# Pooled attention and two MoE layers on one core: the float32 value products of two key tiles issued together

## The chip, the cores and the metric

The kernel runs on one core of a Trainium2 chip. The metric is the device time of one execution in microseconds; less is better. The engines of the core work side by side, each with its own queue in program order, and meet at semaphores: TensorE (PE; its weight loads appear as PEld), VectorE (DVE), ScalarE (ACT), GpSimd (POOL) and SyncE (SP), which here issues the DMAs.

## What is computed

Four batches of eight heads, 1152 keys, head size 64. Pairs of neighbouring queries are averaged, so a head has 576 queries. Then two MoE-like layers follow on the 2304 tokens of 512 features.

```python
def _attn_ref(q, k, v):
    q_pool = q.reshape(B, H, S // 2, 2, D).mean(axis=3)
    scores = scale * np.matmul(q_pool, k.transpose(0, 1, 3, 2))
    scores = scores - np.max(scores, axis=-1, keepdims=True)
    attn = np.exp(scores)
    attn = attn / (np.sum(attn, axis=-1, keepdims=True) + 1e-09)
    return np.matmul(attn, v)

def reference(...):
    x = attn_out.transpose(0, 2, 1, 3).reshape(B * S, H * D)   # S = 576 here
    x = _moe_ref(x, w_in, w_out)      # h = x @ w_in; g = h - tanh(h); g @ w_out
    return _moe2_ref(x, ...)          # g = h * sigmoid(1.702 h)
```

## The kernel before, in words

**Tiles.** The 32 heads are worked on in 16 pairs. A head's keys are nine tiles of 128 (t = 0 to 8), its 576 queries two halves of 288. A loop of 288 steps (`g`, 18 to a pair, nine to a head) computes for one key tile the scores, and three steps later (`LAG = 3`) that tile's products with the values. In this text step i of a pair is `g % 18`, and m = 0 to 8 is the step of a head counted by its value products: m = 0 is step 3 of a pair for the even head and step 12 for the odd one; m = 4 is step 7 or 16.

**Precision.** Most products are fp32r, and what one of them loses is made up by a second and third one: a value v is held as `vh + vl`, a probability p as `ph + pl`, and `vh*ph`, `vl*ph` and `vh*pl` are accumulated: six products for a tile (three parts, two halves). Every third tile (`whole(t)`, t = 1, 4, 7) instead multiplies float32 by float32 in one go (L469, `vfs` by `pf`): two products for a tile, no `ph` and no `pl`.

**One step, in order of issue.** (1) `scores(g)`: four products (L433, L434) into one of two PSUM tiles `sc`; ACT then writes `pf` (L439) and, for a tile that isn't whole, `ph` (L449). (2) `max_at[g]`: two products into the PSUM tile `mx` (L327), for the maxima of the next pair's queries; VectorE reduces `mx` (L331). The pool `ps_mx` has one buffer, so the next step's two products wait for this reduction. In steps with two such jobs the second comes after the value products. The last pair has none. (3) `rest(g - 1)`: `pl = pf - ph` of the tile before, on VectorE (L457), or on GpSimd in steps 5 and 14 of a pair's tiles (others in pair 0, none in the last pair). (4) `pv(g - 3)`: the value products of one tile. (5) the jobs of `plan` (`opening` for pair 0): among them `max_rows` in steps 3 and 13 (VectorE, L390 and L392, then DMAs), `prep_ql` in step 14 (VectorE, L294), `prep_kl` in steps 16 and 17 (GpSimd, L307), `prep_qs` in step 17 (VectorE, L283). (6) from pair 8 on, conversions of the MoE weights (`early`): in pairs 8, 10, 12 and 13 VectorE's L138 in step 6 and L158 in step 15.

Program order is the order in which each engine runs its part. PSUM is full: four banks of `sc`, two of `mx`, two of value accumulators `pv`. Buffers in SBUF: `pf` five, `ph` four, `pl` three.

Of the kernel before, what the change touches and what calls it, by code (L numbers as in the profile page):

```python
# [7 lines left out]
F32 = mybir.dt.float32  # L8
# [20 lines left out]
def tile_pooled_attention_two_moe(  # L29
# [13 lines left out]
    B, NPB, _, S = k.shape  # L43
    NT, DM = out.shape
    D = 64
    SP = S // 2
    HB = SP // 2
    KT = S // 128
# [163 lines left out]
    def attention(ctx: ExitStack):  # L212
        ap = ctx.enter_context(tc.tile_pool(name="attn", bufs=1))
# [15 lines left out]
        def whole(t):  # L229
            return t % 3 == 1  # L230
# [190 lines left out]
        probs, accs, halves = {}, {}, {}  # L421

        def scores(g):
            hd, t = divmod(g, KT)
            a1, a2, q2, q3 = stacks[hd % 3]
            pf = ap.tile([128, SP], F32, tag="pf", name="pf", bufs=5)
            ks = slice(128 * t, 128 * t + 128)
            sc = ps_sc[g % 2].tile([128, 2, 512], F32, tag="sc", name="sc")
            for x in range({1: 2, 2: 2, 3: 1}.get(g, 0)):
                nc.tensor.matmul(sc[:, x], *zeros, start=True, stop=True)  # L430
            for x in range(2):
                xs = slice(x * HB, (x + 1) * HB)
                nc.tensor.matmul(sc[:, x, 0:HB], a1[:, ks], q2[:, xs], start=True, stop=False)  # L433
                nc.tensor.matmul(sc[:, x, 0:HB], a2[:, ks], q3[:, xs], start=False, stop=True)  # L434

            def both(tile):
                return tile.rearrange("p (x i) -> p x i", x=2)

            nc.scalar.activation(both(pf), sc[:, :, 0:HB], AF.Exp, scale=SCALE)  # L439
            if whole(t):  # L440
                probs[g] = None, None, pf
                return
            ph = ap.tile([128, SP], F32R, tag="ph", name="ph", bufs=4)
            pl = ap.tile([128, SP], F32R, tag="pl", name="pl", bufs=3)
            if g in pool_cast:
                nc.gpsimd.tensor_scalar(
                    out=ph, in0=pf, scalar1=1.0, scalar2=1.0, op0=ALU.mult, op1=ALU.mult)
            else:
                nc.scalar.activation(both(ph), sc[:, :, 0:HB], AF.Exp, scale=SCALE)  # L449
            probs[g] = ph, pl, pf  # L450

        def rest(g):
            ph, pl, pf = probs[g]
            if ph is None:
                return
            eng = nc.gpsimd if g % NS in pool_sub.get(g // NS, (5, 14)) else nc.vector
            eng.tensor_tensor(pl, pf, f32(ph[:]), op=ALU.subtract)  # L457

        def pv(g):
            hd, t = divmod(g, KT)  # L460
            p, s = divmod(hd, 2)
            ph, pl, pf = probs.pop(g)
            vh, vl = vt[hd % 3]
            if t == 0:
                accs[hd] = [
                    ps_pv.tile([128, HB], F32, tag=f"pv{x}", name=f"pv{x}") for x in range(2)]
            if ph is None:
                for x in range(2):
                    nc.tensor.matmul(  # L469
                        accs[hd][x], vfs[hd % 3][:, t // 3, :], pf[:, x * HB:(x + 1) * HB],  # L470
                        start=False, stop=False)
                return
            order = [(n, x) for n in range(3) for x in range(2)]
            if t in (0, KT - 1):
                order.sort(key=lambda nx: nx[1])
            parts = (vh, ph), (vl, ph), (vh, pl)
            for n, x in order:
                w, r = parts[n]
                nc.tensor.matmul(  # L479
                    accs[hd][x], w[:, t, :], r[:, x * HB:(x + 1) * HB],  # L480
                    start=(t == 0 and n == 0), stop=(t == KT - 1 and n == 2))
            if t == KT - 1:
                u = wpool.tile([128, SP], F32, tag="u", name="u", bufs=3)
                for x in range(2):
                    nc.scalar.activation(u[:, x * HB:(x + 1) * HB], accs[hd][x], AF.Copy)  # L485
                halves[hd] = u
# [3 lines left out]
        def sums(p):  # L490
            ua, ub = halves.pop(2 * p), halves.pop(2 * p + 1)
            s9 = wpool.tile([128, QJ], F32, tag="s9", name="s9", bufs=2)
            nc.sync.dma_start(
                out=s9[0:64, :], in_=ua[64:65, :].rearrange("o (p i) -> o p i", i=QJ))
            nc.sync.dma_start(
                out=s9[64:128, :], in_=ub[64:65, :].rearrange("o (p i) -> o p i", i=QJ))
            norm[p] = dict(ua=ua, ub=ub, s9=s9)

        def recip(p):
            s9 = norm[p]["s9"]  # L500
            r9 = wpool.tile([128, QJ], F32, tag="r9", name="r9", bufs=2)
            nc.gpsimd.tensor_scalar(
                out=r9, in0=s9, scalar1=1.0, scalar2=1e-9, op0=ALU.mult, op1=ALU.add)
            nc.vector.reciprocal(r9, r9)
            norm[p]["r9"] = r9
# [32 lines left out]
        LAG = 3  # L538
# [19 lines left out]
                lambda c=c: split_x(0, [c], nc.gpsimd if c < 2 else nc.vector))  # L558

        low, high = slice(0, 64), slice(64, 128)  # L560
        qa, ka = [ap.tile([128, SP], F32, tag="pf", name="pf", bufs=5) for _ in range(2)]
        nc.sync.dma_start(out=qa, in_=first[0])
        nc.sync.dma_start(out=ka, in_=first[1])
        load_q(0, high)
# [92 lines left out]
        for n in range(1, NPAIR):  # L657
            for h in range(2 * QJ):
                g = NS * n - 14 + h
                if h < 8 and n == 1:  # L660
                    g = (6, 7, 8, 9, 9, 10, 11, 11)[h]
# [27 lines left out]
        for g in range(total + LAG):  # L689
            p, i = divmod(g, NS)  # L690
            if g < total:
                scores(g)
            if g == LAG:
                ps_two.close()
                ps_mx = ctx.enter_context(tc.tile_pool(name="ps_mx", bufs=1, space=PSUM))
                ps_pv = ctx.enter_context(tc.tile_pool(name="ps_pv", bufs=1, space=PSUM))
            two = max_at.get(g, ())
            for job in two[:1] if g >= LAG else two:
                job()
            if 0 < g <= total:  # L700
                rest(g - 1)
            if g >= LAG:
                pv(g - LAG)
                for job in two[1:]:
                    job()
            for o in range(4):
                if p + o < NPAIR:
                    for fn, *args in (plan if p else opening).get((o, i), ()):
                        fn(p + o, *args)
            if 0 < p < NPAIR:  # L710
                if i == 4:
                    sums(p - 1)
                elif i == 8:
                    recip(p - 1)
                elif i == 9:
                    merge(p - 1)
                elif i == 14:
                    spread(p - 1)
            if p > 1 and i in (2, 5):
                normalise(p - 2, [i // 3])  # L720
            for go in early.pop((p, i), ()):
                go()
# [251 lines left out]
```

## Time and profile before

| | us |
|---|---|
| median of three runs (lowest, highest) | 1305.24 (1302.64, 1306.35) |
| the profiled execution | 1305.66 |
| its span, first to last instruction | 1303.9 |
| TensorE busy in the span | 1292.7 |
| VectorE, ACT, GpSimd busy | 986.1, 754.0, 361.6 |

Attention takes about the first 505 us, the two MoE layers the rest. A profile gives each instruction's start and length. Products are pipelined: a product's recorded length is longer than its distance to the next one, and its end is modelled. The distance between the starts of like products of neighbouring steps is the better measure of a step.

### The profile page before, as it was taken

How to read it: one execution, taken by the hardware profiler on the slowest of the kernel's cores; microseconds unless marked ns; L12 is line 12 of the kernel's file. 1: busy time of each engine (PE TensorE's matmuls, PEld its weight loads, DVE VectorE, ACT ScalarE, POOL GpSimd, SP SyncE). 2: the span in 40 equal slices, each digit the busy share in tenths (PEclk: the TensorE clock that was granted, in tenths of full speed). 3: DMA queues.
4: the chain of work that ended last, by engine and by line, in shares of the span. 5: the costliest groups of instructions: out<-in, count | busy, mean ns of one | idle time of the engine just before them, and what ended most of it. 6: DMA issues, size and time to landing. Idle time of an engine off the chain costs nothing.

```text
span 1303.9 us, 18915 instructions
## 1 busy us (share of the span) xinstructions
PE 1292.7 (99%) x7043; PEld 1155.5 (89%) x7043; DVE 986.1 (76%) x1277; ACT 754.0 (58%) x1159; POOL 361.6 (28%) x277
## 2 busy tenths in 40 slices
PE   9999999999999999999999999999999999999998
PEld 6899999999999999889889889889889889889887
DVE  5777777888879888999999999999944645645433
ACT  5777777777777767787666665665543322322211
POOL 6633333344334323224332332332100100100000
PEclk7999999999999999999999999999999999999999
DMA  7666666766767531211111111111211111111012
GB/s 189 169 152 160 180 172 162 171 170 167 186 170 181 136 95 35 60 46 50 50 33 49 49 33 46 36 33 50 65 35 47 49 33 50 49 33 33 25 41 80
DMA packets 58739, 116.25 MB, mean 89 GB/s; under 512 B 24856, under 2 KB 28952, under 8 KB 58648
## 3 DMA queue, kind: packets, MB, share of 16 engines
q1 hardware_dynamic: 58648, 115.05, 33.9%
q8 instruction: 55, 0.90, 0.3%
q14 instruction: 36, 0.29, 0.1%
HBM read 66.58 MB, written 4.79 MB: 55 GB/s over the span
## 4 chain that ended last, share of the span: by engine, by line
PE 76%; DVE 13%; ACT 6%; issue 2%; POOL 1%; DMA 1%; DVEq 0%; SPq 0%; POOLq 0%; ACTq 0%
PE y L850 21%; PE h L755 20%; PE pv L479 11%; PE pv L469 7%; PE sc L434 6%; PE sc L433 5%; PE mx L327 5%; DVE gg L813 2%; DVE gg L796 2%; ACT u L794 2%; DVE wt L144 1%; DVE wt L138 1%; DVE xb L870 1%; DVE wt L158 1%; ACT a L815 1%
## 5 line engine op out<-in xcount | busy, mean ns | idle before, releaser
L331 DVE TENSOR_REDUCE mt<-mx 128x1 fp32r<-128x576 f32 x270 | 203.6, 754 | 83.3 <-PE mx L327 78.9
L439 ACT ACTIVATE pf<-sc 128x576 f32<-128x576 f32 x288 | 188.5, 655 | 127.9 <-PE sc L434 117.5
L755 PE MATMUL h<-hl,big 128*128 128x512 f32 (+1 forms) x940 | 211.6, 377 | 0.0
L755 PEld LDWEIGHTS h<-hl,big 128*128 128x128 f32 x940 | 174.0, 188 | 28.6
L850 PE MATMUL y<-g,big 128*128 128x512 f32 (+1 forms) x780 | 185.3, 368 | 1.5 <-POOL g L767 1.3
L433 PE MATMUL sc<-q,big 128*128 128x288 f32 x576 | 184.5, 333 | 0.1
L850 PE MATMUL y<-big,g 128*128 128x512 f32 x702 | 181.0, 390 | 0.0
L166 POOL TENSOR_TENSOR big<-wt,big 128x512 fp32r<-128x512 f32 x46 | 61.4, 1334 | 379.7 <-ACT big L165 379.7
L434 PE MATMUL sc<-q,a 65*128 65x288 f32 x576 | 164.8, 300 | 0.0
L850 PEld LDWEIGHTS y<-g,big 128*128 128x128 f32 x780 | 142.6, 188 | 21.5 <-POOL g L767 3.1
L765 ACT ACTIVATE g<-gg 128x1024 fp32r<-128x1024 f32 (+1 forms) x80 | 78.0, 975 | 138.5 <-DVE gg L826 76.3
L850 PEld LDWEIGHTS y<-big,g 128*128 128x128 f32 x702 | 131.6, 188 | 27.1
L479 PE MATMUL pv<-ph,big 128*128 128x288 f32 x768 | 142.5, 296 | 0.9 <-ACT u L485 0.9
L870 DVE TENSOR_TENSOR xb<-xb,y 128x512 f32<-128x512 f32 (+1 forms) x114 | 72.1, 655 | 86.7 <-PE y L850 86.7
L457 DVE TENSOR_TENSOR pl<-pf,ph 128x576 fp32r<-128x576 f32 x159 | 132.7, 835 | 2.2 <-ACT ph L449 1.5
L755 PE MATMUL h<-hl,w 128*128 128x512 f32 (+1 forms) x564 | 127.0, 377 | 0.0
L449 ACT ACTIVATE ph<-sc 128x576 fp32r<-128x576 f32 x188 | 122.8, 653 | 0.0
L755 PEld LDWEIGHTS h<-hl,w 128*128 128x128 f32 x564 | 104.4, 188 | 17.1
L327 PE MATMUL mx<-kh,big 128*128 128x288 f32 x540 | 117.9, 300 | 1.0 <-DVE mt L331 0.6
L479 PEld LDWEIGHTS pv<-ph,big 128*128 128x128 f32 x768 | 116.7, 189 | 1.7 <-issue 0.7
L433 PEld LDWEIGHTS sc<-q,big 128*128 128x128 f32 x576 | 110.5, 192 | 5.9 <-ACT ph L449 0.5
L815 ACT ACTIVATE a<-u 128x1024 f32<-128x1024 f32 (+1 forms) x40 | 39.1, 978 | 132.3 <-DVE gg L813 132.3
(126 smaller groups left out, 2225.4 us busy)
## 6 DMA issues: line engine op xcount, KB each, us to landing
raw<-in_moe_w_in_dram SPq DMA_DIRECT2D x32, 512.0 KB
raw<-in_moe_w_out_dram SPq DMA_DIRECT2D x32, 512.0 KB
big<-kh SPq DMA_DIRECT2D x31, 288.0 KB
q<-qh SPq DMA_DIRECT2D x62, 144.0 KB
big<-kl SPq DMA_DIRECT2D x31, 288.0 KB
a<-kh SPq DMA_DIRECT2D x31, 288.0 KB
kr<-in_k_dram SPq DMA_DIRECT2D x15, 576.0 KB
qr<-in_q_dram SPq DMA_DIRECT2D x15, 576.0 KB
```

Source lines behind the costliest of these rows:

```text
L327: nc.tensor.matmul(mx[:, a, 0:n], bdqs[p % 2][:, 128 * j:128 * j + 128], d["kh"][:, k0:k0 + n], start=True, stop=True)
L331: nc.vector.tensor_reduce(d["mt"][:, c:c + 1], mx[:, :, 0:n], AX.XY, ALU.max, negate=True)
L433: nc.tensor.matmul(sc[:, x, 0:HB], a1[:, ks], q2[:, xs], start=True, stop=False)
L434: nc.tensor.matmul(sc[:, x, 0:HB], a2[:, ks], q3[:, xs], start=False, stop=True)
L439: nc.scalar.activation(both(pf), sc[:, :, 0:HB], AF.Exp, scale=SCALE)
L449: nc.scalar.activation(both(ph), sc[:, :, 0:HB], AF.Exp, scale=SCALE)
L457: eng.tensor_tensor(pl, pf, f32(ph[:]), op=ALU.subtract)
L469: nc.tensor.matmul(accs[hd][x], vfs[hd % 3][:, t // 3, :], pf[:, x * HB:(x + 1) * HB], start=False, stop=False)
L479: nc.tensor.matmul(accs[hd][x], w[:, t, :], r[:, x * HB:(x + 1) * HB], start=(t == 0 and n == 0), stop=(t == KT - 1 and n == 2))
L755: nc.tensor.matmul(hb[:, j, 0:TBS[b]], wi[:, c, w, :], x[r][c], start=(k == 0), stop=(k == 3 * NKC - 1))
L850: nc.tensor.matmul(ys[m][:, 0:w], lhsT, rhs, start=(fp == 0 and not low and j == p == 0), stop=(fp == 1 and low and j == 1))
L870: nc.vector.tensor_add(dst, dst, ys[m][:, 0:w])
```

## The change

The value products of a head are no longer issued tile by tile. A table `pv_order` says for each of a head's nine steps which tiles' parts are issued. Step 1 issues the first two parts of tile 2, step 2 the float32 products of tiles 1 and 4 one after the other, step 3 the last part of tile 2 and the first of tile 3, step 4 the last two parts of tile 3. Steps 0 and 5 to 8 are as before. So tile 2 begins one step earlier, tile 1 comes one step later, and tile 4 two steps earlier, one step after its scores. `probs` keeps a tile's buffers until its last part. The five `pf` buffers become two (`pw`, whole tiles) and three (`pf`, the others).

```diff
-            pf = ap.tile([128, SP], F32, tag="pf", name="pf", bufs=5)
+            if whole(t):
+                pf = ap.tile([128, SP], F32, tag="pw", name="pw", bufs=2)
+            else:
+                pf = ap.tile([128, SP], F32, tag="pf", name="pf", bufs=3)
...
-        def pv(g):
+        pv_order = (
+            ((0, 0, 3),), ((2, 0, 2),), ((1, 0, 3), (4, 0, 3)), ((2, 2, 3), (3, 0, 1)),
+            ((3, 1, 3),), ((5, 0, 3),), ((6, 0, 3),), ((7, 0, 3),), ((8, 0, 3),),
+        )
+
+        def pvs(g):
+            hd, m = divmod(g, KT)
+            for t, n0, n1 in pv_order[m]:
+                pv(hd * KT + t, n0, n1)
+
+        def pv(g, n0, n1):
...
-            ph, pl, pf = probs.pop(g)
+            ph, pl, pf = probs.pop(g) if n1 == 3 else probs[g]
...
-            order = [(n, x) for n in range(3) for x in range(2)]
+            order = [(n, x) for n in range(n0, n1) for x in range(2)]
...
-        qa, ka = [ap.tile([128, SP], F32, tag="pf", name="pf", bufs=5) for _ in range(2)]
+        qa, ka = [ap.tile([128, SP], F32, tag="pf", name="pf", bufs=3) for _ in range(2)]
...
-                pv(g - LAG)
+                pvs(g - LAG)
```

## Rows read from the trace of the kernel before

**Rows 1.** The page: span and instructions.
```profile
span 1303.9 us, 18915 instructions
```
**Rows 2.** Steady attention: stretch, length, busy by PE, PEld, DVE, ACT, POOL, clock, DMA.
```profile
60.00:475.00 415.00, 414.87 (x2831) 396.33 (x2830) 340.24 (x529) 306.53 (x546) 144.82 (x127) 1.00 0.68 165
```
**Rows 3.** Waits of PE in the whole run: total us, times, longest.
```profile
PE pv L479 <- ACT u L485: 0.9, 2, 0.5
PE mx L327 <- DVE mt L331: 0.6, 2, 0.3
```
**Rows 4.** Groups by line and form, float32 products: busy us, mean ns of one.
```profile
L469 PE MATMUL pv<-pf,vf 128*128 128x288 f32 x252 | 71.4, 406 | 0.0
```
**Rows 5.** Timeline, PE, two neighbouring steps: start, length, instruction, count.
```profile
305.19 0.43 PE L327 MATMUL mx<-kh,big 128*128 128x288 f32 x2
...
306.79 0.42 PE L327 MATMUL mx<-kh,big 128*128 128x288 f32 x2
307.05 1.13 PE L469 MATMUL pv<-pf,rbd 128*128 128x288 f32 x4
...
308.56 0.43 PE L327 MATMUL mx<-kh,big 128*128 128x288 f32 x2
```
**Rows 6.** Timeline, DVE, pair 0, reductions close together; idle before in brackets.
```profile
42.97 0.76 DVE L331 TENSOR_REDUCE mt<-mx 128x1 fp32r<-128x576 f32 x1 [0.35 <-PE mx L327]
44.35 0.76 DVE L331 TENSOR_REDUCE mt<-mx 128x1 fp32r<-128x576 f32 x1 [0.62 <-PE mx L327]
45.73 0.76 DVE L331 TENSOR_REDUCE mt<-mx 128x1 fp32r<-128x576 f32 x1 [0.62 <-PE mx L327]
```
**Rows 7.** Timeline, DVE, steps 3 and 4 of pairs 7, 2 and 14.
```profile
240.62 0.76 DVE L331 TENSOR_REDUCE mt<-mx 128x1 fp32r<-128x576 f32 x1 [0.45 <-PE mx L327]
...
242.52 0.72 DVE L331 TENSOR_REDUCE mt<-mx 128x1 fp32r<-128x576 f32 x1
...
91.49 0.76 DVE L331 TENSOR_REDUCE mt<-mx 128x1 fp32r<-128x576 f32 x1 [0.38 <-PE mx L327]
...
93.45 0.72 DVE L331 TENSOR_REDUCE mt<-mx 128x1 fp32r<-128x576 f32 x1
...
450.92 0.76 DVE L331 TENSOR_REDUCE mt<-mx 128x1 fp32r<-128x576 f32 x1 [0.58 <-PE mx L327]
...
452.67 0.72 DVE L331 TENSOR_REDUCE mt<-mx 128x1 fp32r<-128x576 f32 x1
```
**Rows 8.** Timeline, DVE, pair 7, steps 13 to 16.
```profile
257.12 0.76 DVE L331 TENSOR_REDUCE mt<-mx 128x1 fp32r<-128x576 f32 x1
...
258.97 0.76 DVE L331 TENSOR_REDUCE mt<-mx 128x1 fp32r<-128x576 f32 x1
259.65 0.75 DVE L294 TENSOR_TENSOR ql<-qs,qh 128x576 fp32r<-128x576 f32 x1
...
262.77 0.90 DVE L457 TENSOR_TENSOR pl<-pf,ph 128x576 fp32r<-128x576 f32 x1
```
**Rows 9.** Timeline, POOL, pair 7: tile 5's subtraction, even head, odd head, then kl.
```profile
244.99 1.44 POOL L457 TENSOR_TENSOR pl<-pf,ph 128x576 fp32r<-128x576 f32 x1 [3.33 <-ACT ph L449]
...
259.90 1.78 POOL L457 TENSOR_TENSOR pl<-pf,ph 128x576 fp32r<-128x576 f32 x1 [3.52 <-ACT ph L449]
261.65 3.31 POOL L307 TENSOR_TENSOR kl<-kr,kh 128x576 fp32r<-128x576 f32 x2
```
**Rows 10.** Timeline, POOL and DVE, pair 10, steps 14 and 15.
```profile
349.96 1.95 POOL L457 TENSOR_TENSOR pl<-pf,ph 128x576 fp32r<-128x576 f32 x1 [3.14 <-DMA a<-kh]
...
351.25 1.20 DVE L158 SCALAR_TENSOR_TENSOR wt<-raw,wt 128x512 int32<-128x512 int32 x1
```
**Rows 11.** Timeline, ACT and PE, pair 7, odd head: tile 4's exponentials; next maximum products.
```profile
256.86 0.65 ACT L439 ACTIVATE pf<-sc 128x576 f32<-128x576 f32 x1 [0.31 <-PE sc L434]
...
258.43 0.43 PE L327 MATMUL mx<-kh,big 128*128 128x288 f32 x2
```
**Rows 12.** Opening: stretch, length, busy by PE, PEld, DVE, ACT, POOL, clock, DMA.
```profile
17.50:31.20 13.70, 13.70 (x47) 11.03 (x46) 6.12 (x10) 5.23 (x8) 5.88 (x5) 0.50 0.79 199
```

## What the change is predicted to do, and why

> **What bounds the kernel now.** I read the page first, then the busy time by stage, then the waits of TensorE, then single steps in the timeline. The span is 1303.9 us [rows 1] and the profiled execution took 1305.66 us, so 1.8 us lie outside the span; the median shown is 1305.24 us, 0.4 us less, and I carry the sum against 1305.66. In the steady part of attention TensorE is busy 414.87 of 415.00 us at the full granted clock (1.00, the 2.4 GHz level) [rows 2]. Its waits over the whole run are small: 0.6 us for VectorE's maximum, 0.9 us for the copies of the accumulators [rows 3]. So attention lasts as long as its products do. An edit gains only if it makes products cheaper, and it loses whatever time it makes TensorE wait. The MoE stage is not touched and keeps its time.
>
> **What a float32 product costs.** One product is two instructions, 0.406 us each by the mean [rows 4]; four in a row last 1.13 us, so each further one takes (1.13 - 0.406) / 3 = 0.24 us [rows 4, 5]. The distance between the maximum products of neighbouring steps is the time of a step: 305.19 to 306.79 is 1.60 us for twelve fp32r products (0.133 each), 306.79 to 308.56 is 1.77 us for six fp32r and four float32 instructions [rows 5]. 1.77 - 6 x 0.133 = 0.97 = 4 x 0.243. The step of a whole tile is explained by its instructions alone; what is left for the two changes of type around a burst is at most some 0.01 to 0.02 us.
>
> **Bursts joined (gain).** Three bursts in a head become two, 32 fewer in 32 heads. At 0.02 us that is 0.6 us; at nothing, nothing. I take nothing and keep 0.6 us for the low end.
>
> **Products moved.** The head's instructions are the same, in other steps: after the change step m=1 holds four value products in place of the float32 burst, m=2 two bursts, m=3 four products and m=4 four. With six others in each step the distances become 10 x 0.133 = 1.33 us (m=1, 3, 4) and 0.80 + 8 x 0.243 = 2.74 us (m=2). The sum over m=1 to 4 is 6.74 us before and after. What is new is the short step.
>
> **Term A: the floor under a short step.** The maximum's PSUM tile has one buffer: the next two maximum products wait until VectorE's reduction has read it. Where the kernel already issues maximum products with little between, three reductions start at 42.97, 44.35 and 45.73, 1.38 us apart, and VectorE idles 0.62 us before each [rows 6]. That is the shortest cycle: 0.76 us of reduction, then 0.62 us for TensorE to be released and to write again. A step of 1.60 us hides it, a step of 1.33 us doesn't: TensorE waits 0.05 us in each short step, and a wait is not made up, since TensorE has no idle time to give. The Trainium skill, Perfetto Trace Analysis, section Optimizing Tensor Performance, says that independent product groups should rotate through different PSUM banks so that the reading of one overlaps the next; the 1.38 us cycle agrees. Six short steps in each of 15 pairs (the last one has no maximum products) would give 90 x 0.05 = 4.5 us if VectorE were always free. It is not, so I go through the steps in which it is late; the rest counts 0.05 each.
>
> **Term B: step 4 of a pair (m=1, even head).** Here VectorE does a subtraction and the two jobs of max_rows before the reduction. In pair 7 the reductions start at 240.62 and 242.52, 1.90 us apart where 1.60 would be prompt: 0.30 late [rows 7]. Today the following step distance of 1.77 us covers it. With 1.33 us the wait is lateness + reduction (0.72) + 0.62 - 1.33 = 0.31 us. Pair 2 (91.49 to 93.45, 0.36 late) gives 0.37, pair 14 (450.92 to 452.67, 0.15 late) gives 0.16 [rows 7]. The mean of the three, 0.28 us, over 14 pairs: 3.9 us. Steps 6 and 7 (m=3, 4) find VectorE free, since the subtraction of tile 5 is on GpSimd: 2 x 0.05 x 15 = 1.5 us. Pair 0, whose subtractions are slower, some 0.4 us. Even heads: 5.8 us.
>
> **Term C: steps 13 to 17 (odd head), VectorE against GpSimd.** Count from the end of the reduction of step 13 (257.88 in pair 7). VectorE's next reduction starts at +1.09 and the subtraction for ql, on VectorE, at +1.77; GpSimd's subtraction of tile 5 starts at +2.02, after ACT's exponentials of step 14 [rows 8, 9]. Who comes second waits: GpSimd's takes 1.78 us there against 1.44 alone [rows 9], and in pair 10 the integer operation of L158, issued at 351.25 while GpSimd worked until 351.91, ended at 352.45, 0.54 after GpSimd's end [rows 10]. The change brings the scores of step 14 forward by 1.77 - 1.33 = 0.44 us, and GpSimd with them (+1.58), but not VectorE's queue (+1.77). So the order turns round. By hand, pair 7: TensorE waits 0.05 at step 14; GpSimd 1.58 to 3.02; ql until 3.59; the reduction of step 15 from 3.52 to 4.28 instead of 3.37; the maximum products of step 16, due to end at 4.67, end 0.58 after the reduction, 4.86 (wait 0.20); GpSimd's first kl until 4.9, its second until 6.3; VectorE's subtraction of tile 6, issued at 5.58, until 6.87 (today it takes 0.90 us [rows 8]); step 17's maximum products wait 0.05 and its reduction runs 6.80 to 7.56; those of the next step 0, due at 7.84, end at 8.14 (wait 0.30). Together 0.60 us, for the nine pairs among 1 to 13 without weight conversion: 5.4 us. The four with it (8, 10, 12, 13) have L158 too: by the same count 0.21 at step 14 (their reduction of step 13 is 0.18 late), 0.05, 0.49 and 0.30, that is 1.05 us, less 0.35 that they wait today: 2.8 us. Pairs 0 and 14: 0.7 us. Odd heads: 8.9 us.
>
> The Trainium skill, SBUF — State Buffer, section Who interferes with whom, calls the pair of ports that VectorE and GpSimd share an exclusive lock, held for the whole instruction. The trace agrees: 0.54 us after GpSimd's end [rows 10].
>
> If the two queues meet no worse than they do today, term C is 9 x 0.15 (three short steps at 0.05), 4 x 0.6 and 0.4 us for pair 14: 4.2 us.
>
> **What is hidden.** Tile 4's products come one step after its scores. In the odd head its exponentials lie at 256.86 to 257.51 [rows 11], while its burst would begin at some 258.43 - 0.44 + 0.27 + 0.97 = 259.2 (the start of the next maximum products, less the shorter step, then two products and tile 1's burst): 1.7 us of cover; without cover the price is that lateness per head. Tile 2's ph was finished two steps earlier, and its pl is used a step later than now. The split of the pf buffers into two and three keeps at least two steps between last use and next write. No DMA moves, and SyncE's order is the same.
>
> **The opening.** From 17.5 to 31.2 us the granted clock is 0.50 (1.2 GHz) with TensorE busy 13.70 of 13.70 us [rows 12]. Head 0's first burst now lies in it at twice the price; moved a step later it may fall behind the rise, while four fp32r products take its place. That is worth up to 4 x 0.24 - 4 x 0.13 = 0.4 us; should the rise come 2 us earlier or later, 1 us. I take nothing and keep 1.5 us both ways.
>
> **Sum.** 5.8 + 8.9 = 14.7 us: 1305.66 + 14.7 = 1320.4, say 1320.
>
> **Rivals.** (1) The queues keep their present order or the collisions of term C are milder: 5.8 + 4.2 = 10 us, 1315.7. For it: the order turns on a margin of 0.19 us. Against: the lateness of B is in the trace already. (2) Lateness passes on: the 0.20 and 0.30 us waits of C also occur in heads that I counted as free, through VectorE's other jobs; another 0.5 us in each of 15 pairs: 1328. (3) The other side, not slower: the change of type has a price that the ends, being modelled, hide. If a burst's instructions took as little as fp32r ones (0.133), 0.97 - 0.53 = 0.44 us of each burst would be hand-over, and 32 x 0.44 = 14 us would come back: 1306 against the main sum, 1302 against rival 1. It decides once a burst's hand-over exceeds 14.7 / 32 = 0.46 us (0.31 against rival 1). Against it: the 0.24 us inside the burst, where no type changes [rows 4, 5]. (4) The change does nothing to the waits, since VectorE's reduction would find its tile in time: no loss, 1305. The 1.38 us cycle speaks against it [rows 6].
>
> **How the numbers follow.** Main case 0.48, rival 1 0.28, rival 2 0.13, rival 3 0.06, rival 4 0.05. The predicted time is the main one's, 1320. The range: from rival 1 less 1.5 us of opening, 0.6 us of bursts and 2 us for lateness smaller than counted (1311) to rival 2 (1328). Some 0.3% (3.9 us) is about what a measurement of this kernel tells from no change. Slower by more: 0.89, the first three; within: 0.07; faster: 0.04, both from rivals 3 and 4.
>
> **What the profile after would show.** A wait of TensorE's maximum products for VectorE's reduction (0.6 us in all now) of some 10 to 15 us, in small pieces after steps of m=1, 3 and 4; distances of 1.38 us or more there and some 2.74 us at m=2; bursts of eight float32 instructions 0.243 apart; in odd heads ql longer than 0.75 us and GpSimd's subtraction near 1.44; the MoE stage as long as now. Wrong if the distances at m=1, 3 and 4 are 1.33 us without waits, or if the instruction after a burst comes earlier than the count of instructions allows.

## The result and the profile after

The changed kernel takes 1322.74 us, median of four runs (1322.17 to 1323.38); the kernel before takes 1303.94 us in the same comparison (1300.59 to 1306.35). The ratio is 1.015, with a 95% interval of 1.0128 to 1.0171: slower, by 18.8 us of medians. The profiled executions give 1323.38 against 1305.66 us, 17.7 us apart, and spans of 1321.4 against 1303.9 us. The forecast was 1320, range 1311 to 1328.

Where did the time go? Cut both traces at the first scoring product of pair 1 and at that of pair 15. These two rows are the cuts in the profile after (start, length, instruction):

```profile
57.63 0.29 PE L436 MATMUL sc<-q,big 128*128 128x288 f32 x1
...
492.59 0.29 PE L436 MATMUL sc<-q,big 128*128 128x288 f32 x1
```

In the profile of before they lie at 55.29 and 474.79 us. So the span comes apart like this:

| | before, us | after, us | difference |
|---|---|---|---|
| up to pair 1 (opening and pair 0) | 55.29 | 57.63 | +2.34 |
| pairs 1 to 14, "the steady stretch" | 419.50 | 434.96 | +15.46 |
| pair 15, to the end of attention | 29.97 | 29.79 | -0.18 |
| the MoE stage | 799.12 | 799.04 | -0.08 |

All of it is in attention, nearly all in the steady stretch. The table of stretches for exactly that stretch (length, busy time of PE, PEld, DVE, ACT, POOL, granted clock, DMA share, GB/s) reads, first before, then after:

```profile
55.29:474.79 419.50, 419.32 (x2858) 400.26 (x2857) 343.88 (x534) 308.70 (x550) 147.81 (x129) 1.00 0.68 166
```
```profile
57.63:492.59 434.96, 431.51 (x2858) 402.25 (x2857) 360.87 (x535) 307.66 (x549) 143.55 (x128) 1.00 0.65 160
```

The clock is 1.00 in both, and TensorE has exactly 2858 instructions in both. After, it counts as busy for 431.51 of 434.96 us. Read alone, that says "still bound by its products", and it misleads: the products are the same and take 15 us longer. Most of a wait stands inside the busy time, because records overlap: a product's record lasts 0.29 us where the next product starts 0.133 us later, so the first 0.16 us of a wait lie under the record of the product before, and the records of the two products behind a wait last up to 0.53 us in place of 0.43. The view of waits shows more of it (engine, line, waited for: us in the whole run, times, longest), first before, then after:

```profile
PEld mx L327 <- DVE mt L331: 3.1, 9, 0.6
```
```profile
PEld mx L327 <- DVE mt L331: 16.9, 54, 1.1
...
PE mx L327 <- DVE mt L331: 4.0, 11, 0.8
```

The second row stood at 0.6 us before [rows 3]. The two rows are not to be added up: a long wait of a product stands in its weight load's row a second time, and the many short waits stand in neither. What they show is who is waited for, VectorE's reduction. How much is waited follows from the distances of like products, below. The row of the float32 products shows that they cost what they cost in [rows 4], 0.406 us of record each:

```profile
L482 PE MATMUL pv<-pw,vf 128*128 128x288 f32 x252 | 67.9, 406 | 0.0
```

The even head of pair 7, first TensorE, then VectorE, answers to [rows 5 to 7]:

```profile
248.51 0.43 PE L327 MATMUL mx<-kh,big 128*128 128x288 f32 x2
...
250.11 0.43 PE L327 MATMUL mx<-kh,big 128*128 128x288 f32 x2
...
251.63 0.53 PE L327 MATMUL mx<-kh,big 128*128 128x288 f32 x2
252.00 2.10 PE L482 MATMUL pv<-pw,vf 128*128 128x288 f32 x8
```
```profile
248.97 0.76 DVE L331 TENSOR_REDUCE mt<-mx 128x1 fp32r<-128x576 f32 x1 [0.44 <-PE mx L327]
249.65 0.97 DVE L460 TENSOR_TENSOR pl<-pf,ph 128x576 fp32r<-128x576 f32 x1
250.54 0.15 DVE L390 TENSOR_TENSOR mt<-mt 128x5 fp32r<-128x5 f32 x1
250.72 0.21 DVE L392 STREAM_TRANSPOSE tt<-mt 128x32 f32<-128x32 f32 x1
250.86 0.72 DVE L331 TENSOR_REDUCE mt<-mx 128x1 fp32r<-128x576 f32 x1
...
252.20 0.76 DVE L331 TENSOR_REDUCE mt<-mx 128x1 fp32r<-128x576 f32 x1
...
254.94 0.76 DVE L331 TENSOR_REDUCE mt<-mx 128x1 fp32r<-128x576 f32 x1 [1.65 <-PE mx L327]
256.32 0.76 DVE L331 TENSOR_REDUCE mt<-mx 128x1 fp32r<-128x576 f32 x1 [0.62 <-PE mx L327]
```

The reader is to see three things. The reduction at 250.86 starts 1.89 us after the one at 248.97, since a subtraction and the two operations of max_rows stand before it: the lateness of [rows 7], unchanged. TensorE comes to the end of its now shorter step while that reduction still runs, until 251.58: the records of the next maximum products start at 251.63 and last 0.53 us in place of 0.43. And the last two reductions lie 1.38 us apart with VectorE idle for 0.62 us before the second: the floor of [rows 6] in a plain step. The eight float32 instructions last 2.10 us, so each after the first takes (2.10 - 0.406) / 7 = 0.242 us.

### The profile page after: what moved, and what is told of

Read it like the earlier page. It is cut to its first block, busy times and chain, and to the rows that moved or that the text cites. A ratio compares the mean times of both kernels' runs of the same rounds, so it can differ in the third digit from the quotient of the medians.

```text
span 1321.4 us, 18916 instructions
## 1 busy us (share of the span) xinstructions
PE 1306.1 (99%) x7043; PEld 1158.3 (88%) x7043; DVE 1003.7 (76%) x1277; ACT 753.5 (57%) x1159; POOL 357.0 (27%) x277
## 4 chain that ended last, share of the span: by engine, by line
PE 69%; DVE 16%; ACT 6%; DMA 3%; issue 3%; SPq 2%; POOL 1%; DVEq 0%
PE y L863 21%; PE h L768 20%; PE pv L492 8%; PE pv L482 6%; PE mx L327 5%; PE sc L437 4%; PE sc L436 4%; DVE gg L826 3%; DVE mt L331 2%; DVE gg L809 2%; ACT u L807 2%; DVE wt L144 1%; SPq L400 1%; ACT a L828 1%; DMA rbd<-rd 1%
## 5 line engine op out<-in xcount | busy, mean ns | idle before, releaser
L442 ACT ACTIVATE pf<-sc 128x576 f32<-128x576 f32 x192 | 125.9, 656 | 122.8 <-PE sc L437 122.1
L436 PE MATMUL sc<-q,big 128*128 128x288 f32 x576 | 177.1, 320 | 0.0
L492 PE MATMUL pv<-ph,big 128*128 128x288 f32 x768 | 147.9, 297 | 0.8 <-ACT u L498 0.8
L460 DVE TENSOR_TENSOR pl<-pf,ph 128x576 fp32r<-128x576 f32 x159 | 135.8, 854 | 1.6 <-ACT ph L452 1.5
L327 PE MATMUL mx<-kh,big 128*128 128x288 f32 x540 | 124.6, 312 | 5.3 <-DVE mt L331 4.0
```

The lines of the kernel that those rows point to most:

```text
L327: nc.tensor.matmul(mx[:, a, 0:n], bdqs[p % 2][:, 128 * j:128 * j + 128], d["kh"][:, k0:k0 + n], start=True, stop=True)
L492: nc.tensor.matmul(accs[hd][x], w[:, t, :], r[:, x * HB:(x + 1) * HB], start=(t == 0 and n == 0), stop=(t == KT - 1 and n == 2))
```

## Experiments

All are built on the kernel after unless the text says otherwise. Where "distance" is said, it is from the start of the second of a step's two maximum products to that of the next step's second one, since the record of the first begins some 0.1 us early behind a wait; in the merged rows shown here, the ends (start plus length) give the same. TensorE's wait is what a distance has over the time of the step's products. The steady stretch was cut in each profile at the same two products as above.

| kernel | steady stretch, us | median, us | ratio to before (95%) |
|---|---|---|---|
| before | 419.50 | 1303.94 | - |
| after | 434.96 | 1322.74 | 1.015 (1.0128 to 1.0171) |
| after, once more (r_after) | 435.06 | 1318.52 | 1.0132 (1.0109 to 1.0154) |
| after, short reductions (e1_after_short) | 417.20 | 1301.12 | 0.9991 (0.9976 to 1.0007) |
| before, short reductions (e1_before_short) | 418.35 | 1300.11 | 0.999 (0.998 to 1.0001) |
| before, buffers split (e6_buffers) | 419.35 | 1301.58 | 0.9992 (0.9975 to 1.0009) |
| bursts one step apart (e7_apart) | 424.73 | 1308.55 | 1.0056 (1.0033 to 1.0079) |
| max_rows a step later (e2_rows) | 431.97 | 1316.05 | 1.009 (1.0066 to 1.0115) |
| ql a step earlier (e4_ql) | 427.03 | 1309.77 | 1.0051 (1.0032 to 1.0069) |
| kl cut short (e3_kl_short) | 426.46 | 1308.64 | 1.0049 (1.0033 to 1.0066) |
| these three together (e5_three) | 422.84 | 1308.87 | 1.0035 (1.0018 to 1.0052) |
| even spread (e9_flat_only) | 430.59 | 1314.19 | 1.0093 (1.0065 to 1.0122) |
| even spread, max_rows and ql moved (e8_flat) | 425.43 | 1308.0 | 1.0047 (1.0032 to 1.0062) |
| the same, kl cut short (e10_flat_kl) | 419.51 | 1303.47 | 1.0012 (0.9999 to 1.0025) |

Each ratio is to the kernel before as it ran beside that kernel: its median there was 1301.47 to 1301.92 us in all rows below the second. The medians scatter by some 4 us with the clock of the opening (last section), so the steady stretch is the sharper measure. The expectations below reckon from the 1322.74 us of the kernel after, whose four runs all have a mean granted clock of 0.994 to 0.996; most runs of the other kernels have 0.998 to 1.00 and come out some 4 us lower by that alone.

**Is the wait for the reduction the whole loss, and does joining the bursts bring anything? (e1_after_short, e1_before_short.)** The same edit in both kernels: the reduction reads 32 of its 576 columns, so the maxima are those of part of the keys.

```diff
-                d["mt"][:, c:c + 1], mx[:, :, 0:n], AX.XY, ALU.max, negate=True)
+                d["mt"][:, c:c + 1], mx[:, :, 0:16], AX.XY, ALU.max, negate=True)
```

> The changed kernel, with VectorE's reduction of the maximum products reading 16 columns of each half instead of 288 (so the maxima are those of a part of the keys). The reduction becomes short and the one PSUM tile of the maximum comes free early. Theory (the one-buffer cycle of 1.38 us and VectorE's late queue make the whole loss): the distances of the short steps fall to 1.33 us, the waits go, and the time is within 2 us of the kernel before with the same short reduction, some 1301 to 1304 us. Rival, other waits (tile 4 close behind its scores, buffers split in two and three, ACT): the time stays 10 us or more above it. Rival, hand-over between the two product types has a price: it comes out below it, by up to 14 us.

> The kernel before with the same short reduction (16 columns of each half), for comparison with the changed one. Theory: 1300 to 1304 us, since TensorE waits for the reduction only a few us in all. Both rivals expect the same of this one; they differ in the other.

Measured: 1301.12 and 1300.11 us; steady stretches of 417.20 and 418.35 us, the second with one wait of 0.8 us in pair 1 that the first doesn't have. The 15.46 us are gone. TensorE and VectorE in the odd head of pair 7, changed kernel with short reductions:

```profile
257.58 0.43 PE L327 MATMUL mx<-kh,big 128*128 128x288 f32 x2
...
258.92 0.42 PE L327 MATMUL mx<-kh,big 128*128 128x288 f32 x2
...
260.25 0.43 PE L327 MATMUL mx<-kh,big 128*128 128x288 f32 x2
```
```profile
258.05 0.19 DVE L331 TENSOR_REDUCE mt<-mx 128x1 fp32r<-128x32 f32 x1 [1.89 <-PE mx L327]
259.38 0.19 DVE L331 TENSOR_REDUCE mt<-mx 128x1 fp32r<-128x32 f32 x1 [1.14 <-PE mx L327]
```

The reduction takes 0.19 us, and the short steps are 1.34 and 1.33 us long: ten products at 0.133, nothing more. So the whole loss of the steady stretch is the wait for the reduction, and no other wait came with the change. With that wait out of both kernels, 28 heads with two bursts and 28 with three differ by less than 0.5 us once the odd 0.8 us is set aside; a change of type costs no more than some 0.01 to 0.02 us per burst. The rival that gave the hand-over a price of 0.44 us falls.

**The buffers alone (e6_buffers).** The kernel before, with the five pf buffers split into two and three as in the change, and nothing else.

```diff
-            pf = ap.tile([128, SP], F32, tag="pf", name="pf", bufs=5)
+            if whole(t):
+                pf = ap.tile([128, SP], F32, tag="pw", name="pw", bufs=2)
+            else:
+                pf = ap.tile([128, SP], F32, tag="pf", name="pf", bufs=3)
```

> The kernel before with only the five pf buffers split into two for whole tiles and three for the others; the order of the products as before. Theory: no change, 1302 to 1306 us. Rival (the split makes ACT or the products wait): slower, in part or all of the 17 us.

1301.58 us, ratio 0.9992; 419.35 us of steady stretch against 419.50. The split is hidden, as counted.

**The bursts one step apart (e7_apart).** The float32 products are not joined: tile 1's burst returns to m=1, and all else stays where the change puts it.

```diff
-            ((0, 0, 3),), ((2, 0, 2),), ((1, 0, 3), (4, 0, 3)), ((2, 2, 3), (3, 0, 1)),
+            ((0, 0, 3),), ((2, 0, 2), (1, 0, 3)), ((4, 0, 3),), ((2, 2, 3), (3, 0, 1)),
```

> The changed kernel, but the burst of tile 1 goes back into step m=1, behind the four products of tile 2, and step m=2 holds the burst of tile 4 alone: three bursts in a head again, and the only short steps are m=3 and m=4. Theory: the wait at step 4 of a pair (3.9 us) and those of step 13 go, GpSimd and VectorE keep their present order in step 14; left are the two short steps with 0.05 each (3 us) and the meetings at L158 and kl in four pairs: 1308 to 1312 us. Rival, joined bursts are worth something in themselves: this one loses that gain, so it is no faster than the changed kernel (1322).

1308.55 us and 424.73 us of steady stretch: of the 15.46 us lost, 5.2 are left. The step of m=1 is now 2.30 us long and covers the late reduction: no wait after steps 4 and 13. The short steps left (6, 7, 15, 16) are 1.38 us each, which makes 14 x 4 x 0.05 = 2.8 us. Most of the rest is the odd heads, where kl (3.34 us from 261.70) now catches qs, which takes 1.32 us, and a wait of 0.19 us follows step 0 of the next pair; that one was not expected. So what costs is which step is short where VectorE is late, not the joining.

**max_rows one step later (e2_rows).** Term B alone: the two operations that stand before the reduction of step 4 go behind the next one.

```diff
-            (0, 3): [(max_rows, 1)],
+            (0, 4): [(max_rows, 1)],
```

> The changed kernel with the odd head's row jobs of VectorE (max_rows, two short instructions) issued one step later, in step 4 of a pair instead of step 3, so that they no longer stand ahead of the reduction of step 4. Theory (a wait is lateness + reduction + 0.62 us less the step): the distance after step 4, now 1.45 to 1.70 us, falls to 1.38 to 1.44 in pairs 1 to 14; 2.7 us less than the changed kernel, about 1320. Rival (VectorE simply has too much work in the short steps, in whatever order): nothing changes, the row jobs cost their time one step later, 1322 to 1323.

The steady stretch falls by 2.99 us (435.0 to 431.97), the distances of step 4 from 1.45 to 1.70 down to 1.38 to 1.41. The term stands.

**ql one step earlier (e4_ql).** Term C: VectorE's ql gets ahead of GpSimd's subtraction of tile 5, instead of behind it.

```diff
-            (2, 14): [(prep_ql,), (load_v, 1)],
+            (2, 13): [(prep_ql,)], (2, 14): [(load_v, 1)],
```

> The changed kernel with VectorE's subtraction for ql issued in step 13 instead of step 14, so that it comes before GpSimd's subtraction of tile 5 and not behind it. Theory (the order of the two at step 14 turned round): the distance after step 15, now 1.52 us in the pairs without weight conversion, falls to 1.38, and that after step 17, now 1.91, to some 1.70, since GpSimd's kl ends earlier against VectorE's subtraction of tile 6; 3.5 us less, about 1319. Rival (the blocking has nothing to do with ql's place): the distances stay, 1322 to 1323; or VectorE's queue only gets longer at step 13 and the distance after it grows, 1324.

1309.77 us; the steady stretch falls by 7.9 us, more than twice what was expected. VectorE and GpSimd in pair 7:

```profile
259.34 0.71 DVE L294 TENSOR_TENSOR ql<-qs,qh 128x576 fp32r<-128x576 f32 x1
...
263.85 0.95 DVE L460 TENSOR_TENSOR pl<-pf,ph 128x576 fp32r<-128x576 f32 x1
```
```profile
260.01 1.41 POOL L460 TENSOR_TENSOR pl<-pf,ph 128x576 fp32r<-128x576 f32 x1 [3.07 <-ACT ph L452]
261.38 2.81 POOL L307 TENSOR_TENSOR kl<-kr,kh 128x576 fp32r<-128x576 f32 x2
```

ql takes 0.71 us in place of 1.83, and that carries on: nothing of VectorE's lies in GpSimd's way, so kl ends after 2.81 us in place of 3.34, and the subtraction of tile 6 behind it takes 0.95 in place of 1.33. Step 15 is 1.38 us (1.52 in the kernel after); step 17 is 1.59 in place of 1.91, that is, without wait (in the pairs with weight conversion it stays at 1.90); step 16 of pairs with weight conversion is 1.38 in place of 1.82, and step 0 of pairs 9, 11 and 13 is 1.60 in place of 2.33. The expectation left step 17 with 0.1 us and did not count the last two: one collision moves the queues behind it by a whole chain.

**kl cut short (e3_kl_short).** From the other end: GpSimd's two kl operations do 16 of 576 columns each from pair 2 on, and the rest of kl is not written.

```diff
-                kl=ap.tile([128, S], F32R, tag="kl", name="kl"),
+                kl=kl_one,
...
-            xs = slice(x * SP, (x + 1) * SP)
+            xs = slice(x * SP, x * SP + (SP if p < 2 else 16))
```

> The changed kernel with GpSimd's two subtractions for kl cut to 16 of 576 columns each from pair 2 on (the other columns keep what was there, so the low part of the keys is left out of the true computation). ql and tile 5's subtraction stay where they are. Theory (GpSimd's kl blocks VectorE's subtraction of tile 6 and L158): the distance after step 17, now 1.90, falls to 1.60, that after step 16 in pairs 8, 10, 12 and 13 from 1.82 to 1.38, that after the following step 0 from 2.32 to 1.60; the one after step 15 stays at 1.52: some 8 us less, about 1315. Rival (VectorE is late by its own work alone): the distances stay and with them the time, 1322.

The steady stretch falls by 8.5 us, as expected. In pair 7 (line numbers two higher):

```profile
260.39 1.83 DVE L296 TENSOR_TENSOR ql<-qs,qh 128x576 fp32r<-128x576 f32 x1
...
264.19 0.75 DVE L462 TENSOR_TENSOR pl<-pf,ph 128x576 fp32r<-128x576 f32 x1
```

ql is late as before (it waits for the subtraction of tile 5, not for kl), and step 15 keeps its 1.52 us; the subtraction of tile 6 is prompt, and steps 16, 17 and 0 lose their waits. So there are two collisions one after the other, and the second hangs on when kl starts.

**All three (e5_three).** max_rows and ql moved and kl cut short as above: what is left when these three no longer make VectorE late.

> The changed kernel with all three: row jobs one step later, ql one step earlier, kl cut to 16 columns from pair 2 on (that part of the computation is left out). Theory: VectorE is free at every short step, and what remains is the floor alone, 1.38 us in place of 1.33 in six steps of each pair: 4.5 us above the kernel before in the steady part, 1306 to 1310 in all. Rival (no floor; all waits come from lateness): the distances of the short steps fall to 1.33 and the time to that of the kernel before, 1302 to 1304.

422.84 us, 3.3 us over before; 1308.87 us. In pair 7 every short step is at the floor:

```profile
259.35 0.76 DVE L333 TENSOR_REDUCE mt<-mx 128x1 fp32r<-128x576 f32 x1 [1.07 <-PE mx L329]
260.73 0.76 DVE L333 TENSOR_REDUCE mt<-mx 128x1 fp32r<-128x576 f32 x1 [0.62 <-PE mx L329]
...
262.11 0.76 DVE L333 TENSOR_REDUCE mt<-mx 128x1 fp32r<-128x576 f32 x1
```

1.38 us twice, with 0.62 us of idle VectorE. 14 x 6 x 0.05 = 4.2 us is the floor's price. Less the 1.9 us that the kernel before waits itself, plus two waits of 0.37 us after step 9 of pairs 1 and 9, plus 0.16 us more than the floor after step 13 of the five pairs with weight conversion (pair 14 converts weights too), that makes 3.8 us, against 3.3 measured; the bursts' 0.3 to 0.4 us of the first pair of experiments are about the rest.

**No short step at all (e9_flat_only, e8_flat, e10_flat_kl).** If the floor and the lateness are the loss, a head that keeps its joined burst, but has five to a step of the fp32r products in m=0, 1, 3, 4, 5 and 6 rather than six or four, should lose the floor's part: eleven products are 1.46 us, over 1.38.

```diff
-            ((0, 0, 3),), ((2, 0, 2),), ((1, 0, 3), (4, 0, 3)), ((2, 2, 3), (3, 0, 1)),
-            ((3, 1, 3),), ((5, 0, 3),), ((6, 0, 3),), ((7, 0, 3),), ((8, 0, 3),),
+            ((0, 0, 5),), ((0, 5, 6), (2, 0, 4)), ((1, 0, 6), (4, 0, 6)),
+            ((2, 4, 6), (3, 0, 3)), ((3, 3, 6), (5, 0, 2)), ((5, 2, 6), (6, 0, 1)),
+            ((6, 1, 6),), ((7, 0, 6),), ((8, 0, 6),),
...
-            order = [(n, x) for n in range(n0, n1) for x in range(2)]
+            order = [(n, x) for n in range(3) for x in range(2)]
...
-            for n, x in order:
+            for n, x in order[n0:n1]:
```

This alone:

> The same even spread of eleven products a step, without moving the row jobs and ql. Theory: the floor goes (0.05 in each short step), but lateness stays: in step 4 of a pair the reduction is late by 0.44 instead of 0.30, since step 3 is shorter too, so the wait there stays near 0.28 us; in odd heads 0.10 after step 15 and 0.33 after step 17; some 10 to 13 us above the kernel before, 1311 to 1315. Rival (the floor was the main loss): near the kernel before, 1302 to 1306.

1314.19 us, 430.59 us of steady stretch: the floor is gone, the lateness stays (step 4 at 1.60 to 1.83 us, step 15 at 1.58, step 17 at some 1.83). With max_rows and ql moved as in the two kernels above, the lateness should go too:

> Joined bursts, but the 36 fp32r value products of a head spread evenly: five in each of the steps m=0, 1, 3, 4, 5 and 6, six in m=8 (the burst pair in m=2, tile 7's in m=7 as before), so that the shortest step has eleven products, 1.47 us, above the 1.38 us cycle; with it the row jobs one step later and ql one step earlier, as in the two runs before. The whole computation is there. Theory: no floor is touched and VectorE is in time, except where L158 and kl meet in four pairs; joining itself costs and gains nothing: within 3 us of the kernel before, 1301 to 1305. Rival (joined bursts cost something of their own, through ACT's scores or long steps): 1308 or more. Rival (joining gains, hidden so far by the waits): 1298 or less.

It came to 1308.0 us, over the 1301 to 1305 expected. The distances are 1.46 us in most short steps, as they should be. The main exception is step 17: 1.46 to 2.47 us, different from pair to pair. Smaller ones are step 13 of the pairs with weight conversion (1.68 us), step 16 of pairs 8 and 12, and single steps of pairs 1, 7, 9 and 12. VectorE and GpSimd in pair 5, one of the worst:

```profile
201.97 1.86 DVE L460 TENSOR_TENSOR pl<-pf,ph 128x576 fp32r<-128x576 f32 x1
203.75 0.74 DVE L331 TENSOR_REDUCE mt<-mx 128x1 fp32r<-128x576 f32 x1
```
```profile
198.09 1.41 POOL L460 TENSOR_TENSOR pl<-pf,ph 128x576 fp32r<-128x576 f32 x1 [3.08 <-ACT ph L452]
200.40 2.82 POOL L307 TENSOR_TENSOR kl<-kr,kh 128x576 fp32r<-128x576 f32 x2 [0.89 <-DMA big<-kl]
```

GpSimd is free at 199.50 and starts kl at 200.40: it waits for the DMA that still reads the kl of the pair before. 0.89 us later than in a pair without that wait, kl meets VectorE's subtraction of tile 6, which takes 1.86 us instead of the 0.75 of e3_kl_short. The theory had kl's start follow from GpSimd's own queue; here a landing sets it. If the meeting with kl is what is left, the same kernel with kl cut short has no such wait:

> The even spread with the row jobs one step later and ql one step earlier, as before, and GpSimd's two subtractions for kl cut to 16 of 576 columns from pair 2 on (the low part of most keys is left out). The even spread with the full kl took 1308 us, 3 us more than was expected at most: in its trace kl starts 3.4 to 4.3 us after the scores of step 14, when a DMA that reads the previous kl has landed, and VectorE's subtraction of tile 6 stands behind it. Theory (that meeting is all that was left; joined bursts neither cost nor gain): the distances after step 17 fall to 1.47 us, and the time to that of the kernel before or a little less, 1299 to 1303. Rival (joined bursts or the even spread cost something of their own): it stays at 1306 or more. Rival (joining gains, hidden so far): 1297 or less.

```profile
198.63 0.76 DVE L333 TENSOR_REDUCE mt<-mx 128x1 fp32r<-128x576 f32 x1 [0.71 <-PE mx L329]
199.31 0.75 DVE L462 TENSOR_TENSOR pl<-pf,ph 128x576 fp32r<-128x576 f32 x1
200.09 0.76 DVE L333 TENSOR_REDUCE mt<-mx 128x1 fp32r<-128x576 f32 x1
```

In pair 5 the subtraction takes 0.75 us, the reductions are 1.46 us apart, the steady stretch is 419.51 us and the median 1303.47, 0.5 us over the range expected (six of its twelve runs have the low clock of the opening; the other six take 1300.64 to 1302.62 us) and, at 1.0012 (0.9999 to 1.0025), not to be told from the kernel before. What waits are left are 0.21 us at step 13 of the five pairs with weight conversion, 0.07 us at step 4 of pairs 2 to 5, and 0.77 and 0.38 us at step 9 of pairs 1 and 9. With nearly every wait of the change taken away, the joined bursts give nothing back that the time shows: the most that a version of this idea reached is the time of before, and this one leaves part of kl out. No kernel that does the whole computation was faster than before beyond the intervals of the table.

**The kernel after once more (r_after).** To see how far its time repeats.

> The changed kernel once more, unaltered, in the same rounds as the kernel before and the two even spreads. Theory: 16 to 18 us above the kernel before where both run their opening at the same granted clock; the kernel before lies between 1300 and 1306 by the clock of its opening, so the same 4 to 6 us should be seen in this one.

1318.52 us against 1301.47, +17.05 us; its steady stretch is 435.06 us, 0.1 us from the first profile. Its runs stand in two groups, 1317.9 to 1318.5 and 1321.8 to 1322.8 us, and those of e5_three too, 1304 to 1306 and 1309 to 1311; the last section shows what lies behind such groups.

## Why the prediction was right, and where it was not

**The joined bursts bring nothing.** Taken at nothing, with up to 0.6 us of gain for the low end. The two kernels with short reductions bear it out, and the instructions of a burst of eight are 0.242 us apart, as those of a burst of four are.

**The short steps and the floor (term A).** Right, though [rows 6] have the idle 0.62 us only before the second and third reduction (0.35 us before the first): 1.33 us by the products (e1_after_short shows it bare), 1.38 us wherever VectorE is prompt, 0.05 us lost each time. Steps 6 and 7 sum to 1.43 us over pairs 1 to 14, 1.4 by the forecast; m=2 is 2.74 us long, as forecast.

**Step 4 (term B).** 3.81 us over pairs 1 to 14; the forecast was 3.9. Its three pairs came close to the mean of the fourteen: the distance is 1.46 us in pair 1, 1.70 in 2 to 5, 1.62 in 6 to 9, 1.56 in 10 to 13, 1.50 in pair 14, against 1.70, 1.64 and 1.49 from its three.

**The order that turns (term C).** The step that the forecast called least certain held in pair 7 almost to the hundredth. GpSimd first, then VectorE, odd head:

```profile
268.20 1.40 POOL L460 TENSOR_TENSOR pl<-pf,ph 128x576 fp32r<-128x576 f32 x1 [3.08 <-ACT ph L452]
269.56 3.34 POOL L307 TENSOR_TENSOR kl<-kr,kh 128x576 fp32r<-128x576 f32 x2
```
```profile
265.87 0.76 DVE L331 TENSOR_REDUCE mt<-mx 128x1 fp32r<-128x576 f32 x1
...
267.71 0.76 DVE L331 TENSOR_REDUCE mt<-mx 128x1 fp32r<-128x576 f32 x1
268.39 1.83 DVE L294 TENSOR_TENSOR ql<-qs,qh 128x576 fp32r<-128x576 f32 x1
270.14 0.74 DVE L331 TENSOR_REDUCE mt<-mx 128x1 fp32r<-128x576 f32 x1
271.51 0.76 DVE L331 TENSOR_REDUCE mt<-mx 128x1 fp32r<-128x576 f32 x1 [0.62 <-PE mx L327]
272.18 1.33 DVE L460 TENSOR_TENSOR pl<-pf,ph 128x576 fp32r<-128x576 f32 x1
273.44 0.74 DVE L331 TENSOR_REDUCE mt<-mx 128x1 fp32r<-128x576 f32 x1
```

Count again from the end of step 13's reduction, 266.63. GpSimd's subtraction starts at +1.57 (forecast +1.58) and ends at +2.97; ql starts at +1.76, behind it, and ends at +3.59 (forecast +3.59); the reduction of step 15 runs from +3.51 (+3.52); kl ends at +6.27 (+6.3); the subtraction of tile 6 ends at +6.88 (+6.87); step 17's reduction runs from +6.81 (+6.80). In [rows 8, 9] the roles were the other way round: ql 0.75 us, GpSimd 1.78. The waits came to 0.05, 0.19, 0.05 and 0.31 us for a forecast of 0.05, 0.20, 0.05 and 0.30, and in pairs with weight conversion to 0.21, 0.05, 0.49 and 0.29, for 0.21, 0.05, 0.49 and 0.30. Over pairs 1 to 14, steps 13 to 17 wait 9.85 us, by the forecast 9 x 0.60 + 4 x 1.05 + some 0.35 = 9.95. e4_ql and e3_kl_short show that the cause is this order: each takes one of the two out of the other's way, and the waits behind it go.

The Trainium skill, SBUF — State Buffer, section Who interferes with whom, says that a VectorE instruction with two inputs in SBUF contends with a GpSimd instruction that reads SBUF, and that the order of issue decides who is held. The trace agrees in both orders: ql took 1.83 us when GpSimd was 0.19 us ahead of it, and 0.75 us when it was 0.25 us ahead of GpSimd [rows 8, 9].

**What was missed: step 0 behind weight conversion.** The forecast let the 0.35 us that these pairs wait today vanish. In place of that, step 0 of pairs 9, 11 and 13 grew to 2.33 us. Pair 8 into 9, VectorE, then GpSimd:

```profile
304.67 0.74 DVE L331 TENSOR_REDUCE mt<-mx 128x1 fp32r<-128x576 f32 x1
305.34 1.73 DVE L283 TENSOR_TENSOR qs<-qr 128x576 f32<-128x576 f32 x1
306.99 0.74 DVE L331 TENSOR_REDUCE mt<-mx 128x1 fp32r<-128x576 f32 x1
```
```profile
305.17 1.28 POOL L166 TENSOR_TENSOR w<-wt,w 128x512 fp32r<-128x512 f32 x1 [1.04 <-DMA rbd<-rd]
```

The sum of neighbouring queries (qs, L283) stands behind GpSimd's piece of weight split, begun 0.17 us earlier; the count had GpSimd free after kl. Step 0 waits 2.39 us over pairs 1 to 14 where none was counted. With 0.5 us more of own waits in before than the 4 x 0.35 subtracted, the steady stretch comes to +15.46 us (by the distances 17.48 - 1.92 = 15.56), where the forecast's terms for it make 3.9 + 1.4 + 9.95 - 1.4 = 13.9. The forecast's own sign, 10 to 15 us of waits for the reduction, is exceeded too: 17.48 us by these distances.

**What was missed: pair 0.** Its two terms were some 0.8 us; up to pair 1 it was 2.34 us. Of these, 0.90 us lie ahead of pair 0's first scoring product, which starts at 13.11 us before and at 14.01 after. No step of the sum stands there, and over all the traces of this case that product starts between 13.11 and 14.36 us; that these 0.90 us come from the change is not shown. Pair 0 itself, from its first scoring product to that of pair 1, is 1.44 us longer, and its odd head has 1.40 of them, for a forecast of 0.35. Where the clock of the opening is 1.00 throughout it is much the same: 38.39 us in e4_ql, whose pair 0 is that of the change, against 36.81 us in e6_buffers, whose pair 0 has the order of before. The opening's order is its own: ql comes there in step 15, and stands behind GpSimd just the same (VectorE):

```profile
53.91 1.84 DVE L294 TENSOR_TENSOR ql<-qs,qh 128x576 fp32r<-128x576 f32 x1
```

Step 16 of pair 0 waits 1.1 us for it: the mechanism of term C with twice its price, where the count took pair 0 as one more steady pair. The even head's 0.5 us did not show; its steps lie in part in the stretch at a clock of 0.50, whose place differs in the two profiles. So the 3 us between the forecast and the profiled time are the steady stretch (1.6 us more than its terms), pair 0 (0.6 us more) and the 0.9 us ahead of it: 1305.66 + 2.34 + 15.46 - 0.26 = 1323.2.

**What was hidden stayed hidden.** Tile 4's burst a step after its scores: no wait of the float32 products in the view of waits. The buffers: e6_buffers. The MoE stage: 799.04 us for 799.12.

**The rivals.** That the queues keep their order (1315.7) falls with the rows of pair 7. That lateness passes on to heads counted as free (1328) was right in kind at one place, step 0, with 2.4 us in all and not 0.5 us a pair. That the change of type has a price, or that the waits don't come, fall with the short reductions.

## What to carry to other kernels

Where TensorE is busy all the time, moving products between steps is no neutral act: every step has a floor, set by the turnaround of its single-buffered PSUM tile (here 0.76 us of reduction and 0.62 us to release and refill), and a step cut to under it, or to under the lateness of the engine that reads the tile, loses the difference for good, while the long step that it feeds gains nothing. Compare the distances of like products, step by step, before and after: TensorE's busy share (431.51 of 434.96 us) does not show such waits. And where two engines hold each other up, look by how much one comes first, and what sets that start in either queue, a landing included: here 0.19 us turned an order and cost some 8 us.

## What was unexpected of the hardware

**The clock of the opening.** The stretch at a granted clock of 0.50 (the 1.2 GHz level) in [rows 12] is not there in every execution. The same stretch in the profile of e6_buffers, whose products are those of before, and a like one of the kernel after:

```profile
17.50:31.20 13.70, 12.79 (x77) 10.79 (x78) 9.47 (x15) 10.16 (x17) 8.10 (x7) 1.00 0.78 203
```
```profile
19.90:33.60 13.70, 13.70 (x47) 11.21 (x46) 4.94 (x9) 7.12 (x11) 5.31 (x4) 0.50 0.65 171
```

At 1.00 (the 2.4 GHz level) 77 instructions of TensorE fit where 47 did, and pair 1 begins at 50.68 us in place of 55.29: 4.6 us. Before the fall TensorE was about as busy in both: in the 7.5 us from 10.0 to 17.5 it was 6.20 us busy where the clock then fell, and 6.63 us where it did not. Of the traces here the low stretch is in before, after, r_after and e2_rows (the last two some 10 us of it); in the others it is missing or a few us long. What decides it stays open. It fits the two groups in which the four runs of before stand, 1300.59 and 1302.64 against 1305.24 and 1306.35: of its later runs, those of 1305 us and more have a mean granted clock of 0.995 to 0.997, those of 1300 to 1303 us one of 1.00. With all four runs of the kernel after at 0.994 to 0.996, it also fits that the medians differ by 18.8 us and the profiles, both with the low stretch, by 17.7.

**The change between float32 and fp32r is free** as far as these runs can tell: no more than some 0.01 to 0.02 us per burst.
